# Holding back a load until an earlier load has landed, in a retention and gated feed-forward kernel

## The chip, the cores and the metric

The kernel runs on one core of a Trainium2 chip. The metric is the device time of one execution in microseconds (us), the median of three runs; lower is better. Engines are named as the profile names them: PE (TensorE, its matmuls; PEld are its weight loads), DVE (VectorE), ACT (ScalarE), POOL (GpSimd) and SP (SyncE), which in this kernel issues every transfer. A small q behind an engine's name (SPq) marks its instruction queue: issues and waits that leave the engine itself idle.

## The reference

Two parts, one fed by the other. The first is a linear attention with decay (retention) over 4 batches, 8 heads, 768 tokens and a head dimension of 64:

```python
for t in range(S):
    state = gamma[None, :, None, None] * state + np.einsum('bhd,bhe->bhde', k[:, :, t], v[:, :, t])
    y[:, :, t] = scale * np.einsum('bhd,bhde->bhe', q[:, :, t], state)
```

The second takes that output as `x`, one row of 512 per token:

```python
h = np.maximum(x @ w_in, 0.0)                  # w_in: 512 x 1024
# conv_out: a convolution of h along the sequence, three taps per feature, zero padded
gate = 1.0 / (1.0 + np.exp(-conv_out))
return (h * gate @ w_out).astype(np.float32)   # w_out: 1024 x 512
```

## The kernel before

The retention runs in chunks of 64 tokens: 24 of them (two groups of batches, 12 chunks each), and chunk n computes with one tile `rw[n]` of query, key (in two layouts) and value. `scores/n` multiplies keys by queries on PE, `masked/n` masks the product on DVE, `scale_v/n` scales the values, `mix/n` and `across/n` make the output and the running state on PE, `carry/n` copies the state to the next chunk, `decay/n` finishes the output. Two chunks make a unit of 128 tokens; `x_head`, `x_rest` split its output into two parts, a head rounded to fp32r and a rest, and `mm1/u/f` multiplies a unit by `w_in`. After the convolution and the gate, `mm2` multiplies by `w_out`, and `store` writes the rows.

Weights come as pairs of 32-bit words in 16 loads of 512 KB: `load_w/0` to `load_w/7` bring `w_in`, `load_w/8` to `load_w/15` bring `w_out`, and the small `load_w/16` the taps of the convolution. Each weight is taken apart by a chain of steps on ACT and DVE that begins with `w_abs/i` (ACT, line 481) and `w_clamp/i` (DVE, line 486).

The loads of chunks 0 to 3 are cut in two, `load/n` (query and key, line 335, 512 KB) and `load_kv/n` (key and value, line 339, 512 KB). From chunk 4 on one `load/n` brings 1024 KB. `load_consts` (line 343, 80 KB) and `load_gy` (line 347, 128 KB) bring constants. All loads and stores are issued by SP, in the order in which they stand in a written-out list `ORDER`; an instruction that has to wait on SP keeps all behind it waiting. A load waits for its tile to be free (three tiles `rw`, four tiles `g` for weights). Each transfer signals its landing on one of eight semaphores, DMAHW0 to DMAHW7, taken in turn, and a transfer also waits until the one before it on its semaphore has landed, so that at most eight are in flight. A table `HELD` (line 56) makes seven loads wait for a given compute step as well, `load_kv/2` for `mix/0` and `load_kv/3` for `make_gy/0` among them. PE starts with matmuls on a dummy tile (`fill`, line 318, and `keep_warm`, line 312) while the first loads are on their way.

Of the kernel before, what the change touches and what calls it, by code (L numbers as in the profile page):

```python
# [27 lines left out]
CONV = 2 * NF  # L28
# [20 lines left out]

FILL = 6  # L50
ALONE = 4
SUMMED = 0
BY_SCALAR = (0, 1, 2, 3, 4, 5, 6, 7, 10, 11, 12, 15, 17, 21, 22, 23)


HELD = {
    "load_kv/2": "mix/0", "load_kv/3": "make_gy/0", "load/7": "w_low/4", "load_w/4": "w_abs/3",
    "load_w/6": "w_clamp/5", "load_w/10": "carry/7", "load_w/13": "w_abs/10",
}
# [171 lines left out]
def has_next(n):  # L231
    return ALONE <= n + 1 < N_CHUNKS

# [21 lines left out]
def retention_then_gated_ffn(  # L255
# [36 lines left out]
    def buf(name, shape, dtype=F32):  # L292
        return pool.tile(shape, dtype, **place(name))

    def ps_buf(name, shape=(P, 512)):
        return psum.tile(list(shape), F32, **place(name))


    for i, place_ in enumerate(PLACES.split()):
        name, size = place_.split(":")  # L300
# [7 lines left out]
    def keep_warm(k):  # L308

        ps = ps_buf("ps_o")  # L310
        for i in range(k):
            nc.tensor.matmul(ps[:, : 2 * P], warm, warm.unsqueeze(1).broadcast_to([P, 2, P]), start=True, stop=True)  # L312

    def fill(k):

        ps = ps_buf("ps_o")
        for i in range(k):
            nc.tensor.matmul(ps, warm, warm.unsqueeze(1).broadcast_to([P, 4, P]), start=True, stop=True)  # L318
            made[f"fill/{i}"] = nc.cur_bb.bb.instructions[-1]
# [10 lines left out]
    def load(n):  # L330


        rw[n] = buf("rw", [P, 5, 2, NPAIR, C])
        slots = slice(0, 2 if n < ALONE else 4)
        nc.sync.dma_start(flat(rw[n][:, slots]), qkv[n][:, slots])
# [176 lines left out]
    def w_low(i):  # L512
        low, high, _ = pieces[i]
        out = parts[i] = buf("es", [P, 512], F32R) if i < SUMMED else low.bitcast(F32)
        nc.vector.scalar_tensor_tensor(
# [3 lines left out]
    def w_parts(i):  # L519
        m, es = pieces[i][2], parts[i] if i in parts else None  # L520
        if i < NF:
            fs = slice(i * P, (i + 1) * P)
            m, es = (a if a is None else a.rearrange("p (k f) -> p k f", k=NPAIR) for a in (m, es))
            return wi_hi[:, :, fs], wi_lo[:, :, fs], m, es
        return wo_hi[i - NF], wo_lo.get(i - NF), m, es
# [24 lines left out]
    def w_add(i):  # L550
# [6 lines left out]
        _, lo, m, es = w_parts(i)  # L557
        if i < SUMMED:
            ps = w_ps[i]
# [246 lines left out]
        nc.sync.dma_start(out[r0 : r0 + P, cs], os[u, t, h][:, : cs.stop - cs.start])  # L806

    made = {}
    fill(FILL)
    for name in ORDER.split():  # L810
        if name in WARM:
            keep_warm(WARM[name])
        kind, *args = name.split("/")
        emit[kind](*map(int, args))
        made[name] = nc.cur_bb.bb.instructions[-1]
        if name in HELD:
            tc.add_manual_dep(
                made[name], made[HELD[name]].name,
                mybir.DependencyInfo(mybir.DependencyClass.Sync, mybir.DependencyReason.DATA), reason="held back",
            )  # L820


_OUT = (B * S, DM)
# [48 lines left out]
```

## Time and profile before

| | |
|---|---|
| runs | 334.77, 334.76, 332.27 us; median 334.76 us |
| profiled execution, first to last instruction | 331.0 us |
| PE busy | 322.2 us, 97% of the span |
| DVE busy | 288.7 us, 87% |
| ACT busy | 215.0 us, 65% |
| read from HBM, written to it | 33.79 MB, 6.29 MB |
| TensorE clock granted | full, in every slice |

The page gives the busy time of each engine. The stretches give the same for a part of the span, with the share of the DMA engines. The timeline gives the start and length of single instructions, with the idle time of the engine before them and what ended it. The DMA view, over a short stretch, gives the time from issue to landing of the one transfer issued in it. In the chain of waits each piece is followed back to what released it.

### The profile page before, as it was taken

Reading aid. Unit: us, or ns where it says so; the run is one execution under the profiler, and the core shown is the slowest. Engines: PE = TensorE matmul, PEld = TensorE weight load, DVE = VectorE, ACT = ScalarE, POOL = GpSimd, SP = SyncE. Lnnn points to the kernel's source line nnn. Section 1 sums busy time; section 2 is a strip of 40 time slices with the busy share of each in tenths; the row PEclk is TensorE's granted clock in tenths of the full one; section 3 lists DMA queues with packets and bytes.
Section 4 is the critical chain, followed back from the end, with each engine's and each line's share of the span. In section 5 each row is a group of like instructions: output and inputs, shape, how many; then the busy total and the mean of one; then the engine's idle time right before and its main releaser. Section 6 shows DMA issues by size and latency. Waiting matters only on the chain.

```text
span 331.0 us, 10761 instructions
## 1 busy us (share of the span) xinstructions
PE 322.2 (97%) x4642; PEld 289.4 (87%) x4642; DVE 288.7 (87%) x566; ACT 215.0 (65%) x448; POOL 26.1 (8%) x100
## 2 busy tenths in 40 slices
PE   8888999999999999899999999999999999999996
PEld 3778999999999988798888989999999888987885
DVE  3999999999999999897999998779988887869980
ACT  4657774756666475755939664965796866776761
POOL 0000002003110100300000000021011200120000
PEclk9999999999999999999999999999999999999999
DMA  7999787556443331574150000000000101010111
GB/s 256 386 331 338 251 311 266 197 159 239 180 168 153 130 100 63 160 264 139 51 192 34 34 0 35 34 2 7 25 34 0 64 1 64 3 63 0 65 63 63
DMA packets 10415, 40.77 MB, mean 123 GB/s; under 512 B 1280, under 2 KB 1792, under 8 KB 7808
## 3 DMA queue, kind: packets, MB, share of 16 engines
q1 hardware_dynamic: 10368, 40.09, 34.0%
q8 instruction: 36, 0.59, 0.7%
q14 instruction: 11, 0.09, 0.1%
HBM read 33.79 MB, written 6.29 MB: 121 GB/s over the span
## 4 chain that ended last, share of the span: by engine, by line
PE 94%; DMA 4%; issue 0%; ACT 0%; DVE 0%; ACTq 0%
PE ps_o L793 40%; PE ps_m L576 20%; PE ps_m L696 8%; PE ps_y L696 8%; PE ps_s L396 5%; PE ps_st L396 4%; DMA rw<-in_qkv 4%; PE ps_y L396 4%; PE ps_s L696 3%; PE ps_o L318 2%; PE ps_o L312 0%; ACT rw L364 0%; ACT o_sb L800 0%; DVE o_sb L304 0%; ACTq L800 0%
## 5 line engine op out<-in xcount | busy, mean ns | idle before, releaser
L576 PE MATMUL ps_m<-xu,wi_hi 128*128 128x256 f32 x384 | 68.8, 283 | 0.0
L793 PE MATMUL ps_o<-h,g 128*128 128x512 f32 (+1 forms) x200 | 62.7, 382 | 0.0
L576 PEld LDWEIGHTS ps_m<-xu,wi_hi 128*128 128x128 f32 x384 | 58.4, 189 | 0.9
L576 PE MATMUL ps_m<-xu,wi_lo 128*128 128x256 f32 x192 | 53.5, 279 | 0.0
L764 ACT ACTIVATE cv<-cv 128x512 f32<-128x512 f32 x48 | 29.8, 630 | 34.0 <-DVE cv L758 34.0
L396 PE MATMUL ps_y<-rw 64*64 64x64 f32 x1472 | 48.4, 220 | 0.1
L396 PEld LDWEIGHTS ps_y<-rw 64*64 64x64 f32 x1472 | 45.2, 135 | 0.7 <-ACT rw L629 0.4
L793 PEld LDWEIGHTS ps_o<-h,g 128*128 128x128 f32 x200 | 37.2, 188 | 7.1 <-ACT o_sb L800 0.4
L779 DVE TENSOR_TENSOR g<-cv,g 128x512 fp32r<-128x512 f32 x48 | 32.6, 687 | 8.1 <-ACT g L774 7.4
L758 DVE SCALAR_TENSOR_TENSOR cv<-h,cw_sb,cv 128x256 f32<-128x256 f32 x84 | 38.7, 478 | 1.0 <-ACT cv L753 0.4
L774 ACT CAST g<-cv 128x512 fp32r<-128x512 f32 x48 | 29.3, 617 | 11.7 <-DVE cv L769 10.3
L576 PEld LDWEIGHTS ps_m<-xu,wi_lo 128*128 128x128 f32 x192 | 36.1, 188 | 0.0
L396 PEld LDWEIGHTS ps_s<-rw 64*64 64x64 f32 x768 | 24.4, 135 | 8.6 <-issue 3.2
L396 PE MATMUL ps_s<-rw 64*64 64x64 f32 x768 | 27.6, 221 | 4.0 <-DMA rw<-in_qkv 1.5
L396 PE MATMUL ps_st<-rw 64*64 64x64 f32 x704 | 25.0, 219 | 0.5 <-ACT rw L364 0.5
L364 ACT ACTIVATE rw<-rw,consts_sb 128x128 f32<-128x128 f32 x64 | 20.4, 391 | 6.4 <-DMA rw<-in_qkv 6.4
L396 PEld LDWEIGHTS ps_st<-rw 64*64 64x64 f32 x704 | 22.6, 135 | 1.5 <-ACT rw L364 1.0
L753 ACT ACTIVATE cv<-h,cw_sb 128x256 f32<-128x256 f32 x42 | 20.5, 504 | 2.0 <-DVE g L779 2.0
L800 ACT COPY o_sb<-ps_o 128x512 f32<-128x512 f32 (+1 forms) x25 | 13.9, 561 | 11.8 <-PE ps_o L793 11.7
L423 DVE TENSOR_TENSOR rw<-ps_s,consts_sb 128x512 f32<-128x512 f32 x24 | 16.4, 684 | 5.2 <-PE ps_s L396 5.2
L793 PE MATMUL ps_o<-h_m,g 128*128 128x512 f32 (+1 forms) x50 | 19.1, 384 | 0.0
L793 PE MATMUL ps_o<-h_s,g 128*128 128x512 f32 (+1 forms) x50 | 19.1, 384 | 0.0
(256 smaller groups left out, 758.4 us busy)
## 6 DMA issues: line engine op xcount, KB each, us to landing
rw<-in_qkv SPq DMA_DIRECT2D x20, 1024.0 KB, 5.8
out_y<-o_sb SPq DMA_DIRECT2D x23, 256.0 KB, 2.0
g<-in_w_in SPq DMA_DIRECT2D x8, 512.0 KB, 6.3
rw<-in_qkv SPq DMA_DIRECT2D x8, 512.0 KB, 6.5
g<-in_w_out SPq DMA_DIRECT2D x8, 512.0 KB, 4.7
out_y<-o_sb SPq DMA_DIRECT2D x2, 128.0 KB, 1.7
consts_sb<-in_consts SPq DMA_DIRECT2D x1, 128.0 KB, 8.8
consts_sb<-in_consts SPq DMA_DIRECT2D x1, 80.0 KB, 6.0
```

The costliest lines, as they stand in the source:

```text
L364: nc.scalar.activation(v[:, :, g], v[:, :, g], AF.Copy, scale=by[:, g : g + 1])
L396: nc.tensor.matmul(out, lhsT, rhs, start=start, stop=stop, skip_group_check=True)
L423: nc.vector.tensor_tensor(out=rw[n][:, 1], in0=s_ps[n], in1=mask_sb.unsqueeze(1).broadcast_to([P, 2, NPAIR, C]), op=ALU.mult)
L576: nc.tensor.matmul(h_ps[u, p][:, odd], w[:, k, fs], x[:, k].rearrange("p b t -> p (b t)"), start=(i == 0), stop=(i == len(products) - 1),)
L696: nc.tensor.matmul(ps[:, i], w[k][:, fs], x[:, k].rearrange("p b t -> p (b t)"), start=(i == m == 0 and q in (1, 5)), stop=(m == len(produ ...
L753: nc.scalar.activation(cvs[u, p][:, i], hs[u, p][:, i, :, 1 : P + 1], AF.Copy, scale=cw_sb[:, f, 1:2])
L758: nc.vector.scalar_tensor_tensor(out=cv, in0=h[:, :, k : k + P], scalar=cw_sb[:, f, k : k + 1], in1=cv, op0=ALU.mult, op1=ALU.add)
L764: nc.scalar.activation(cvs[u, p], cvs[u, p], AF.Sigmoid)
L774: nc.scalar.copy(gs[u, p][:, 0], cvs[u, p])
L779: nc.vector.tensor_tensor(out=lo, in0=cvs[u, p], in1=hi.bitcast(F32), op=ALU.subtract)
L793: nc.tensor.matmul(ps, g, w[f][:, cs], start=(f == 0 and i == 0), stop=(f == NF - 1 and i == 2))
L800: nc.scalar.copy(o[:, :n], o_ps[u, t, h][:, :n])
```

## The change

Before a load is issued, SP now also waits for the landing of an earlier load: of the last load that has at least `AHEAD` = 8 units of 128 KB, that is 1 MB, of other loads between itself and the new one. The sizes are in the table `SIZES`: 4 units for 512 KB, 8 for a 1024 KB load, 3 for `load_consts`, 1 for `load_gy`; `load_w/16` counts nothing. Stores are neither held nor counted. The order, the tiles and all other instructions stay.

```diff
+AHEAD = 8
+SIZES = {"load_consts": 3, "load_gy": 1, "load_kv": 4, "load_w": 4, "load": 4}
...
+    def hold(this, by):
+        tc.add_manual_dep(
+            this, by.name, mybir.DependencyInfo(mybir.DependencyClass.Sync, mybir.DependencyReason.DATA),
+            reason="held back",
+        )
+
+    def behind():
+
+        between = 0
+        for load, size in reversed(loads):
+            if between >= AHEAD:
+                return load
+            between += size
...
         if name in HELD:
-            tc.add_manual_dep(
...
+            hold(made[name], made[HELD[name]])
+        if kind in SIZES:
+            landed = behind()
+            if landed is not None:
+                hold(made[name], landed)
+            size = 0 if name == f"load_w/{CONV}" else 8 if kind == "load" and int(args[0]) >= ALONE else SIZES[kind]
+            loads.append((made[name], size))
```

SP at the start of the program, from `load_consts` to `load_kv/2`. Line 343 is `load_consts`, 339 `load_kv`, 463 `load_w`, 335 `load`, 347 `load_gy`; in the changed kernel all numbers are higher by two. DMAHW0 is the landing of `load_w/0`, DMAHW1 of `load_w/1`, and so on in turn. Before:

```order
L343 DMA consts_sb_66<-in_consts 128x160
L339 DMA rw_146<-in_qkv 128x1024
L463 DMA g_2_150<-in_w_in 128x1024
L335 DMA rw_152<-in_qkv 128x1024
L339 DMA rw_152<-in_qkv 128x1024
L347 DMA consts_sb_66<-in_consts 128x256 [waits DMAHW0_49]
L335 DMA rw_156<-in_qkv 128x1024 [waits DMAHW1_49]
L339 DMA rw_156<-in_qkv 128x1024 [waits DMAHW2_49,PE_49]
```

The same place of SP after the change:

```order
L345 DMA consts_sb_66<-in_consts 128x160 [waits DMAHW0_49]
L341 DMA rw_146<-in_qkv 128x1024
L465 DMA g_2_150<-in_w_in 128x1024 [waits DMAHW1_49]
L337 DMA rw_152<-in_qkv 128x1024 [waits DMAHW3_49]
L341 DMA rw_152<-in_qkv 128x1024 [waits DMAHW4_49]
L349 DMA consts_sb_66<-in_consts 128x256 [waits DMAHW5_49]
L337 DMA rw_156<-in_qkv 128x1024
L341 DMA rw_156<-in_qkv 128x1024 [waits DMAHW6_49,DMAHW2_49,PE_49]
```

No row has moved. `load_consts` now waits for `load_w/0`, `load_w/2` for `load_w/1`, `load/1` for `load_consts`, `load_kv/1` for `load_kv/0`, `load_gy` for `load_w/2` (and `load/2` stands behind it), `load_kv/2` for `load/1`.

SP from `load_w/16` to `load_w/5`, before (the names 344 and 450 are `load/4` and `load/5`, 412 and 453 `load_w/4` and `load_w/5`):

```order
L463 DMA cw_t_263<-in_conv_w 128x48 [waits DMAHW5_49]
L339 DMA rw_257<-in_qkv 128x1024 [waits DMAHW6_49,DVE_49]
L335 DMA rw_344<-in_qkv 128x2048 [waits DMAHW7_49,PE_49,Activation_49]
L463 DMA g_0_412<-in_w_in 128x1024 [waits DMAHW0_49,Activation_49]
L335 DMA rw_450<-in_qkv 128x2048 [waits DMAHW1_49,DMAHW2_49,DVE_49,PE_49]
L463 DMA g_1_453<-in_w_in 128x1024 [waits DVE_49]
```

The same place after the change:

```order
L465 DMA cw_t_263<-in_conv_w 128x48 [waits DMAHW2_49]
L341 DMA rw_257<-in_qkv 128x1024 [waits DVE_49]
L337 DMA rw_344<-in_qkv 128x2048 [waits DMAHW3_49,DMAHW7_49,PE_49,Activation_49]
L465 DMA g_0_412<-in_w_in 128x1024 [waits DMAHW6_49,Activation_49]
L337 DMA rw_450<-in_qkv 128x2048 [waits DVE_49,PE_49]
L465 DMA g_1_453<-in_w_in 128x1024 [waits DMAHW0_49,DVE_49]
```

Again no row has moved. `load_w/16` now waits for `load_kv/2` (DMAHW2), and `load_kv/3` stands behind it; `load/4` waits for `load/3` (DMAHW3), `load_w/4` for `load_kv/3` (DMAHW6), and `load_w/5` for `load_w/4` (DMAHW0).

## Rows read from the trace of the kernel before

**Rows 1.** The page, part 1: busy us, share of the span, instructions

```profile
PE 322.2 (97%) x4642; PEld 289.4 (87%) x4642; DVE 288.7 (87%) x566; ACT 215.0 (65%) x448; POOL 26.1 (8%) x100
```

**Rows 2.** Four stretches of the span; the first row names the columns

```profile
core 0: us, PE busy (x) PEld busy (x) DVE busy (x) ACT busy (x) POOL busy (x), PEclk, DMA share, GB/s
10.00:20.00 10.00, 7.65 (x281) 6.62 (x283) 9.35 (x17) 7.81 (x19) 0.00 (x0) 1.00 1.01 371
20.00:26.00 6.00, 4.97 (x123) 4.73 (x117) 5.86 (x12) 2.55 (x8) 0.00 (x0) 1.00 0.99 326
26.00:40.00 14.00, 14.00 (x423) 13.61 (x423) 13.28 (x28) 10.66 (x25) 0.00 (x0) 1.00 0.83 274
40.00:60.00 20.00, 20.00 (x572) 19.42 (x565) 19.50 (x39) 12.45 (x27) 2.06 (x6) 1.00 0.80 294
```

**Rows 3.** The chain of waits, 10 to 32 us: start us, us, what

```profile
11.73 5.07 DMA rw<-in_qkv
...
17.35 8.26 DMA rw<-in_qkv
...
25.75 0.33 PE ps_s L396 x4
```

**Rows 4.** Waits on transfers: who, for what, us in total, times, longest

```profile
ACT rw L364 <- DMA rw<-in_qkv: 6.4, 5, 3.1
ACT m L481 <- DMA g<-in_w_in: 4.6, 4, 2.4
PE ps_s L396 <- DMA rw<-in_qkv: 1.5, 2, 1.0
```

**Rows 5.** Timeline of SP: start us, us, issue of a transfer

```profile
0.74 0.86 SPq L463 DMA_DIRECT2D g<-in_w_in  x2
2.11 0.43 SPq L343 DMA_DIRECT2D consts_sb<-in_consts  x1
3.83 0.45 SPq L335 DMA_DIRECT2D rw<-in_qkv  x1
16.91 0.33 SPq L339 DMA_DIRECT2D rw<-in_qkv  x1
20.19 0.33 SPq L463 DMA_DIRECT2D g<-in_w_in  x1
21.74 0.33 SPq L335 DMA_DIRECT2D rw<-in_qkv  x1
22.12 0.57 SPq L463 DMA_DIRECT2D g<-in_w_in  x1
```

**Rows 6.** DMA view around one issue each: KB, us from issue to landing

```profile
g<-in_w_in SPq DMA_DIRECT2D x1, 512.0 KB, 3.9
consts_sb<-in_consts SPq DMA_DIRECT2D x1, 80.0 KB, 6.0
rw<-in_qkv SPq DMA_DIRECT2D x1, 512.0 KB, 8.1
rw<-in_qkv SPq DMA_DIRECT2D x1, 512.0 KB, 6.2
g<-in_w_in SPq DMA_DIRECT2D x1, 512.0 KB, 6.7
rw<-in_qkv SPq DMA_DIRECT2D x1, 1024.0 KB, 7.6
g<-in_w_in SPq DMA_DIRECT2D x1, 512.0 KB, 8.5
g<-in_w_out SPq DMA_DIRECT2D x1, 512.0 KB, 4.2
g<-in_w_out SPq DMA_DIRECT2D x1, 512.0 KB, 3.3
```

**Rows 7.** Timeline of ACT and of DVE: where the sixth weight block begins

```profile
30.76 0.69 ACT L481 ACTIVATE m<-g 128x512 f32<-128x512 f32 x1
...
31.51 0.42 DVE L486 TENSOR_SCALAR m<-m 128x512 f32<-128x512 f32 x1
```

More of the change, by code (lines that the diff above doesn't have):

```diff
@@ L808, in retention_then_gated_ffn @@
     made = {}
+    loads = []
+    def hold(this, by):
[9 more added lines that the diff above has]
+            between += size
     fill(FILL)
@@ L816, in retention_then_gated_ffn @@
         if name in HELD:
-            tc.add_manual_dep(
-                made[name], made[HELD[name]].name,
-                mybir.DependencyInfo(mybir.DependencyClass.Sync, mybir.DependencyReason.DATA), reason="held back",
-            )
+            hold(made[name], made[HELD[name]])
[5 more added lines that the diff above has]
+            loads.append((made[name], size))
 _OUT = (B * S, DM)
```

## The prediction

> **What bounds the kernel now.** I read the page first, then stretches, the chain of waits, the waits on transfers, and single transfers. The page says that PE is busy 322.2 of 331.0 us [rows 1]: there is little to win but the time in which PE stands. The stretches show where that is: from 10 to 26 us PE works 7.65 of 10 and 4.97 of 6 us, and the DMA engines are at 1.01 and 0.99 of their time; from 26 us on PE is busy throughout and the DMA share falls to 0.83 and 0.80 [rows 2]. The chain agrees: its two pieces of DMA end at 25.6 us, and PE's scores of chunk 4 start behind them at 25.75 [rows 3]. PE waited for transfers twice, 1.5 us in all, once for 1.0 us (the scores of chunk 4); ACT waited 6.4 us for keys and values and 4.6 us for weight blocks [rows 4]. DVE is the second bound: 9.35 of 10, 5.86 of 6, 13.28 of 14 and 19.50 of 20 us [rows 2]. So the kernel is bound by transfers up to 26 us, then by PE with DVE close behind it. What a load loses early stays lost as far as DVE and PE can't catch up.
>
> **What the change adds.** No instruction on PE, DVE, ACT or POOL, no byte, no other order: only waits on SP. I cost SP's waiting itself at nothing. What counts is whether a load that is issued later also lands later.
>
> In the trace loads land in the order of their issue, and under a full queue their issue time doesn't matter: the load of 1024 KB issued at 21.74 lands after 7.6 us, at 29.3, and `load_w/5`, issued at 22.12, after 8.5 us, at 30.6 [rows 5, 6]. That is 1.3 us for 512 KB, the service time. A load could be issued 6 us later and land the same, if its data only stood in the queue. Three loads of 512 KB take 3.8 us of service. With the change a load is issued when the third before it lands, so the three turn around in T, the time from issue to landing with 1 MB in flight; if T is under 3.8 us, nothing is lost.
>
> Which T? The nearest row is `load_kv/2`: held back by `mix/0`, it went out at 11.73 us, when `load/1` (issued 3.83, 8.1 us) was landing at 11.9, so with about 1.1 MB in flight. This is just what the change makes of nearly every early load. It took 5.07 us [rows 3, 5, 6]. `load_kv/3`, issued at 16.91 with 1 MB in flight, took 6.2 us. `load_w/10`, with the 1 MB of `load/10` in flight, took 4.2. With nothing in flight, `load_w/15` took 3.3 and the first load of all 3.9 [rows 5, 6]. So a load that comes late to a working queue takes longer than its share of it; one that is queued early doesn't show this. I take T = 5.1, the row of the same place, between 3.3 and 6.2. Transfer apart, that is 3.8 us of latency under load.
>
> The Trainium skill, page "DMA: Bandwidth & Descriptors", section "Anatomy of one DMA — SWDGE (gpsimd) path", puts a transfer at about 2.0 us fixed plus bytes over 436 GB/s, the fixed part constant; for 512 KB that is an estimate of 3.2 us, and three loads would turn around within their service. By that sum the change costs nothing. The trace agrees for the load on an empty queue (3.3 us) and differs for the one on 1 MB in flight (5.07); the section is also about another issuing path than SP's. The measurement decides.
>
> **The sum.** The longest chain of holds runs from `load_w/0`, landed at 0.74 + 3.9 = 4.6 us, through six loads.
> - `load_consts` is issued at 4.6 instead of 2.11. Its 80 KB take T less 1.1 us of transfer, 4.0: landed 8.6 (before 2.11 + 6.0 = 8.1).
> - `load/1` waits for it: 8.6 + 5.1 = 13.7 (before 11.9, 1.8 us later).
> - `load_kv/2` waits for `load/1`: 18.8 (before 16.8, 2.0 later).
> - `load_w/16` goes with that landing, `load_kv/3` one issue of about 0.5 us behind: 19.3 + 5.1 = 24.4 (before 23.1, 1.3 later; its 6.2 us of before had a delay already).
> - `load_w/4` waits for `load_kv/3`: 29.5 (before 20.19 + 6.7 = 26.9, 2.6 later).
> - `load_w/5` waits for `load_w/4`: 34.6 (before 30.6, 4.0 later).
>
> In general `load_w/5` lands at 4.0 + 6 T. The other chain, `load_w/1`, `load_w/2`, `load_gy`, `load/3`, `load/4`, comes out shorter for `load/4`: 1 MB landed at about 26.4 instead of 25.6. PE arrives later itself by then, so its wait of 1.0 us there is used up; the scores of chunk 4 lose about 1 us.
>
> Who needs `load_w/5`: `w_abs/5` on ACT, which started at 30.76, 0.2 us behind the landing, and took 0.69; `w_clamp/5` on DVE at 31.51 stands behind it [rows 7]. With the block at 34.6, `w_abs/5` ends at about 35.3, and DVE stands 3.8 us later than before. Behind it on DVE, in order, come the second `make_gy` and the mask of the next chunk, for which PE's `mix` waits; behind `w_abs/5` on ACT the first `relu` of the next unit, which frees PE's accumulator. So PE can't run past it. DVE was idle 0.72 us from 26 to 40 and 0.50 from 40 to 60 [rows 2]; these 1.2 us can take up some of it. 3.8 - 1.2 = 2.6 us reach the end.
>
> Later loads: the tiles hold them back already, and `load_w/8`, `load_w/9`, `load_w/14` and `load/16` alone get a later issue. I cost them at nothing: ACT waited for weight blocks four times, at the first, second, fourth and fifth block, and PE twice, the last time at 25.75 [rows 3, 4], so behind these loads stands slack. Without that cover each would cost up to what T exceeds 3.3 by, some 2 us. The stores wait behind the loads on SP but feed nobody.
>
> The span becomes 331.0 + 2.6 = 333.6 us. The median of the runs, 334.76, is 3.8 us above the profiled span (the fastest run 1.3), and 2.6 us on it make 337.4 us, 0.8% slower.
>
> **The rivals.**
> *Hidden.* T is 4.4 or less. With 4.0 + 6 T, `load_w/5` then lands at 30.6 or earlier, as before, and all holds lie under data that stand in the queue. Time 331.0, in the runs 334.8. For it: 4.2 for `load_w/10`, 3.3 on an empty queue [rows 6]. Against it: 5.07 and 6.2 at the very place [rows 3, 6]. The sum of the Trainium skill, above, comes out here.
>
> *Faster.* With less in flight the transfer that is awaited has the DMA engines to itself. `load_kv/3` took 6.2 us while `load/4`, `load_w/4` and the next came in behind it; with T = 4.2 it lands at 17.0 + 4.2 = 21.2 instead of 23.1, and `load/4` two us earlier too. PE's 1.0 us at 25.75 goes: 330.0, in the runs 333.8. It decides the case below T = 4.3. More than 1% needs 3.3 us, and PE's waits on transfers hold 1.5 [rows 4]; only if the runs' spread (332.27 to 334.77) is made by early transfers could more come. Against it: before `load_kv/3`, with more in flight than ever, loads landed 1.3 us apart.
>
> *The start slows down fully.* T = 6.2, the row of `load_kv/3`: `load_w/5` lands at 41.2, 10.6 late, less 1.4 of slack and idle time 9.2 us: 340.2, in the runs 344.0. From T = 5.2 on the loss passes 3.3 us. Against the full figure: when loads land further apart, a late one has more time before its turn, so T falls back.
>
> That the waits are missing is no case: SP's rows show them.
>
> **Chances.** The forecast (0.5 to 3.3 us slower) 0.42; hidden 0.16; faster by less than 1% 0.05, by more 0.05; the start slowed by more than 3.3 us 0.32. A measurement of this kernel tells about 1% from no change. So faster by over 1% 0.05, within 1% 0.63, slower by over 1% 0.32. The range: its low end, 332.8, takes in the hidden case and the faster one (333.8 in the runs) and 1 us of the runs' spread; its high end takes T up to 5.7 (`load_w/5` at 38.2, 7.6 late, 6.2 us at the end, 341.0 in the runs). The forecast's own range is 335.3 to 338.1.
>
> **What would show it.** Right: in the profile of the changed kernel `load/1`, `load_kv/2` and `load_w/5` land at about 13.7, 18.8 and 34.6 us; the DMA share from 10 to 20 us falls from 1.01 to about 0.8; ACT's wait for weight blocks grows from 4.6 us by 3 or more; DVE stands before line 488, the old 486; PE's idle time before 36 us grows by about 2.6. If 512 KB loads with 1 MB in flight land in under 4.4 us, T was too high and the case is *hidden*. If the loads land late and the end doesn't move, DVE and PE had more to give than 1.2 us. If the loss shows after 60 us, one of the four later loads had no cover.

## The result, and the profile after

| | before | changed |
|---|---|---|
| median of four runs beside each other | 334.45 us (332.27 to 334.77) | 337.50 us (336.40 to 337.92) |
| changed / before | | 1.0114, 95% interval 1.0072 to 1.0156 |
| profiled execution | 331.0 us | 335.6 us |

The change makes the kernel slower by 1.1%, 3.8 us by the ratio (2.4 to 5.2), 3.05 us by the medians and 4.6 us by the two profiled executions. The engines run the same instructions. The page of the changed kernel, part 1, against [rows 1]:

```profile
PE 323.6 (96%) x4642; PEld 289.5 (86%) x4642; DVE 288.9 (86%) x566; ACT 214.8 (64%) x448; POOL 27.0 (8%) x100
```

The stretches, with the columns of [rows 2], and one more, from 6 to 10 us, changed and (last row) before:

```profile
10.00:20.00 10.00, 7.43 (x221) 6.06 (x222) 8.26 (x14) 5.43 (x13) 0.00 (x0) 1.00 0.86 295
20.00:26.00 6.00, 4.63 (x155) 4.45 (x151) 4.50 (x9) 3.99 (x11) 0.00 (x0) 1.00 0.89 285
26.00:40.00 14.00, 11.29 (x317) 10.86 (x316) 11.69 (x21) 7.25 (x17) 0.00 (x0) 1.00 0.83 295
40.00:60.00 20.00, 20.00 (x503) 19.41 (x503) 19.86 (x42) 14.23 (x33) 2.06 (x6) 1.00 0.80 285
6.00:10.00 4.00, 4.00 (x40) 2.22 (x39) 2.91 (x7) 1.04 (x2) 0.00 (x0) 1.00 0.82 233
6.00:10.00 4.00, 4.00 (x42) 2.49 (x41) 3.76 (x8) 1.70 (x4) 0.00 (x0) 1.00 0.96 364
```

The DMA engines moved 295 and 285 GB/s from 10 to 26 us where it was 371 and 326, and already from 6 to 10 us only 233 where it was 364. PE is short of work in the stretch up to 40 us, 11.29 of 14 us busy where it was 14.00, and from then on as full as before. From 10 to 40 us it stands 3.3 us more than before; the other 1.3 us of the 4.6 lie in time that the profile counts as busy, 323.6 against 322.2 us. So the loss lies at the start and is then carried along.

The chain of waits of the changed kernel, 5 to 32 us (start us, us, what), against [rows 3]:

```profile
1.17 4.55 DMA g<-in_w_in
...
5.74 6.36 DMA g<-in_w_in
...
12.11 4.61 DMA consts_sb<-in_consts
...
16.79 4.90 DMA rw<-in_qkv
...
21.84 8.46 DMA rw<-in_qkv
...
30.44 0.33 PE ps_s L398 x4
```

These are `load_w/1`, `load_w/2`, `load_gy`, `load/3` and `load/4`, each from the second on issued at the landing of the one above it, and behind them the scores of chunk 4, at 30.44 instead of 25.75. `load/4` itself took 8.46 us, little more than before (8.26, [rows 3]). The scores of chunk 2 were late already; timeline of PE, before and changed:

```profile
16.30 0.27 PE L396 MATMUL ps_s<-rw 64*64 64x64 f32 x2
...
19.31 1.15 PE L398 MATMUL ps_s<-rw 64*64 64x64 f32 x32 [0.96 <-DMA rw<-in_qkv]
```

The waits on transfers, against [rows 4]:

```profile
ACT rw L366 <- DMA rw<-in_qkv: 7.3, 5, 3.5
ACT m L483 <- DMA g<-in_w_in: 7.0, 5, 2.7
PE ps_s L398 <- DMA rw<-in_qkv: 4.1, 3, 2.7
```

PE now waits 4.1 us for query and key instead of 1.5, 2.7 of them for `load/4`. The issues on SP, against [rows 5] (`load_consts`, `load_kv/0`, `load/1`, `load/2`, `load_kv/2`, `load_w/4`, `load_w/5`), and the DMA view of single loads, against [rows 6] (`load_kv/0`, `load_w/2`, `load/1`, `load/2`, `load_kv/2`, `load_w/5`):

```profile
4.49 0.33 SPq L345 DMA_DIRECT2D consts_sb<-in_consts  x1
4.86 0.43 SPq L341 DMA_DIRECT2D rw<-in_qkv  x1
7.22 0.33 SPq L337 DMA_DIRECT2D rw<-in_qkv  x1
12.48 0.43 SPq L337 DMA_DIRECT2D rw<-in_qkv  x1
13.47 0.33 SPq L341 DMA_DIRECT2D rw<-in_qkv  x1
24.96 0.33 SPq L465 DMA_DIRECT2D g<-in_w_in  x1
31.64 0.33 SPq L465 DMA_DIRECT2D g<-in_w_in  x1
```

```profile
rw<-in_qkv SPq DMA_DIRECT2D x1, 512.0 KB, 6.0
g<-in_w_in SPq DMA_DIRECT2D x1, 512.0 KB, 6.4
rw<-in_qkv SPq DMA_DIRECT2D x1, 512.0 KB, 6.2
rw<-in_qkv SPq DMA_DIRECT2D x1, 512.0 KB, 6.7
rw<-in_qkv SPq DMA_DIRECT2D x1, 512.0 KB, 7.0
g<-in_w_in SPq DMA_DIRECT2D x1, 512.0 KB, 4.4
```

`load/2`, the tenth transfer, so landed at 12.48 + 6.7 = 19.2 us. In the kernel before it landed at 5.86 + 9.0 = 14.9, 4.3 us earlier:

```profile
5.86 0.33 SPq L335 DMA_DIRECT2D rw<-in_qkv  x1
```

```profile
rw<-in_qkv SPq DMA_DIRECT2D x1, 512.0 KB, 9.0
```

Where the prediction looked for the sixth weight block, timeline of ACT and DVE, against [rows 7]:

```profile
36.05 0.69 ACT L483 ACTIVATE m<-g 128x512 f32<-128x512 f32 x1 [0.51 <-DMA g<-in_w_in]
...
36.77 0.43 DVE L488 TENSOR_SCALAR m<-m 128x512 f32<-128x512 f32 x1 [0.48 <-ACT m L483]
```

DVE comes there 5.3 us later (36.77 against 31.51), and of that it stands 0.5 us at this place; the rest it brought along.

### The profile page after: what moved, and what is told of

It is laid out like the page before. It is cut to its first block, busy times and chain, and to the rows that moved or that the text cites. A ratio compares the mean times of both kernels' runs of the same rounds, so it can differ in the third digit from the quotient of the medians.

```text
span 335.6 us, 10756 instructions
## 1 busy us (share of the span) xinstructions
PE 323.6 (96%) x4642; PEld 289.5 (86%) x4642; DVE 288.9 (86%) x566; ACT 214.8 (64%) x448; POOL 27.0 (8%) x100
## 4 chain that ended last, share of the span: by engine, by line
PE 90%; DMA 9%; issue 1%; SPq 0%; ACT 0%; ACTq 0%
PE ps_o L795 39%; PE ps_m L578 20%; PE ps_m L698 8%; PE ps_y L698 8%; PE ps_s L398 5%; PE ps_st L398 4%; DMA rw<-in_qkv 4%; PE ps_y L398 4%; DMA g<-in_w_in 3%; PE ps_s L698 3%; DMA consts_sb<-in_consts 1%; SPq L465 0%; ACT o_sb L802 0%; SPq L337 0%; ACTq L802 0%
## 5 line engine op out<-in xcount | busy, mean ns | idle before, releaser
L398 PE MATMUL ps_y<-rw 64*64 64x64 f32 x1472 | 49.1, 220 | 0.0
L366 ACT ACTIVATE rw<-rw,consts_sb 128x128 f32<-128x128 f32 x64 | 20.4, 390 | 7.3 <-DMA rw<-in_qkv 7.3
L755 ACT ACTIVATE cv<-h,cw_sb 128x256 f32<-128x256 f32 x42 | 20.4, 503 | 2.0 <-DVE g L781 2.0
```

The lines of the kernel that those rows point to most:

```text
L366: nc.scalar.activation(v[:, :, g], v[:, :, g], AF.Copy, scale=by[:, g : g + 1])
L398: nc.tensor.matmul(out, lhsT, rhs, start=start, stop=stop, skip_group_check=True)
L755: nc.scalar.activation(cvs[u, p][:, i], hs[u, p][:, i, :, 1 : P + 1], AF.Copy, scale=cw_sb[:, f, 1:2])
```

## The experiments

A hold is a wait of SP for a landing, as the change adds it. Two theories stood against the reading that a chance stall of `load/4` made the loss (B). A: depth. A load that is issued onto 1 MB in flight comes too late, the DMA engines run dry in between. C: waiting on SP costs as such, whatever is in flight. The ratios below are to the kernel before, run beside each; 1% is 3.3 us.

**How much may be in flight.** Three kernels differ from the changed one in one number.

```diff
-AHEAD = 8
+AHEAD = 16      # e1_ahead16: 2 MB in between
+AHEAD = 12      # e7_ahead12: 1.5 MB
+AHEAD = 4       # e2_ahead4: 0.5 MB
```

> The held loads wait as in the changed kernel, but for a load with 2 MB of others in between. Theory A (a load issued onto 1 MB in flight reaches the DMA engines after they have run dry; queue depth is what costs): four loads of 512 KB are still in flight, 5.1 us of service against 5 to 7 us from issue to landing, so nearly nothing is lost: 0 to +1 us on the kernel before, PE idle before 31 us back from 6.6 to about 3.5 us. Theory B (the loss is a chance stall of load/4, which took 8.5 us): unrelated to depth, anything from 0 to +4.6. Theory C (waiting on SP as such costs, since each hold keeps all behind it): nearly as many holds, so +2 to +4 us.

> A load waits for one with 1.5 MB of others in between: four loads of 512 KB in flight at most. Theory A: four loads take 5.1 us of service against 4.5 to 6.5 us from issue to landing, so about a third of the loss: +0.5 to +2 us on the kernel before, between the 2 MB kernel (0.25% above before) and the changed kernel (1.1% above). No other theory puts it between.

> A load waits for one with only 0.5 MB in between, so two loads of 512 KB are in flight instead of three. Theory A: two loads per turnaround of 4 to 5 us, 2.0 to 2.5 us each where 1.3 is the service; load_w/5 lands at 42 to 48 us instead of 36.0, and the time is 6 to 12 us above the changed kernel. Later weight loads (load_w/8, load_w/9, load_w/14) begin to be late too. Theory B: no more than 1 us above the changed kernel. Theory C: about the changed kernel, since the number of holds is the same.

| loads in between | ratio | interval |
|---|---|---|
| 2 MB | 1.0025 | 0.9992 to 1.0059 |
| 1.5 MB | 1.0011 | 0.9979 to 1.0044 |
| 1 MB (the change) | 1.0114 | 1.0072 to 1.0156 |
| 0.5 MB | 1.0362 | 1.0274 to 1.0450 |

With 1.5 and 2 MB the holds are there and cost nothing that can be told; with 1 MB they cost 1.1%, with 0.5 MB 3.6%. That is against C: with 1.5 MB SP did wait, `load/2` was issued at 10.66 instead of 5.86 us and landed at 17.0 instead of 14.9. Against B speak the regular steps, and that `load/4` took hardly longer than before. I had expected 1.5 MB to lose a part; its interval still leaves room for 0.4%. One row of the profiled execution with 0.5 MB says that more than transfers is in the 3.6%: PE was busy 6.06 of 10 us from 10 us on and 4.48 of the next 6, and the granted clock was 0.64 on average in those 6, where it was 1.00 before [rows 2]. All runs with 0.5 MB have a mean granted clock of 0.98 or 0.985, by my estimate at most 5 to 7 us of PE's time out of the 12 us lost.

```profile
20.00:26.00 6.00, 4.48 (x118) 4.32 (x112) 3.63 (x7) 3.41 (x8) 0.00 (x0) 0.64 0.74 235
```

**Which holds.** The holds were limited to a part of the loads, by their place in the order.

```diff
-            if landed is not None:
+            if landed is not None and len(loads) < 10:         # e5_first
+            if landed is not None and 10 <= len(loads) < 19:   # e6_mid
+            if landed is not None and len(loads) >= 19:        # e4_late
+            if landed is not None and len(loads) < 6:          # e10_first_a
+            if landed is not None and 6 <= len(loads) < 10:    # e11_first_b
```

> Only the seven holds from load_consts to load/2 are made; from load_kv/2 on loads are issued as before. In the changed kernel these seven already had load/2 landing 4.3 us later. Theory A (depth): load/2 lands 3 to 4.5 us later than before, the loads behind it queue up deep and catch up a part, +2 to +3.5 us in the end. My prediction's chain put only 1.6 us on load/2: then +1 to +1.5 us. Theory B (the chance stall of load/4 made the loss): 0 to +1.

> Only the nine holds from load_kv/2 to load_w/5 are made; the first ten transfers go out as before, eight in flight. Theory A: up to 14.9 us all loads land as before, then load_w/4 and load_w/5 1 to 3 us later, +1 to +2.5 us in the end. If nearly all of the loss is made here, +3.5 to +4.5, and first holds cost nothing; if none, 0 to +0.5.

> Only the loads from load/6 on are held; the first 19 transfers are issued as before. My prediction's step that the later holds cost nothing: 0, within 0.5 us of the kernel before. Theory C: +1 to +3 us. If load_w/8 or load_w/9 have no cover: +1 to +2 us, with ACT waiting at line 483 after 48 us.

> Only the first three holds are made: load_consts and load_kv/0 on load_w/0, load_w/2 on load_w/1. Theory A (a load that is issued onto 1 MB in flight comes too late, each time anew): these three put load_w/2 1.0 to 1.4 us later, the rest queue up deep behind it and lose no more: +1 to +1.5 us. If the first three make it all, +3.5 to +4.

> Only the four holds on load/1, load_kv/1, load_gy and load/2 are made; the first six transfers go out as before. Theory A: load/2 lands 2 to 3 us later, +1.5 to +3 us in the end; together with the first three holds, the 4 us of all seven.

| holds made | ratio | interval |
|---|---|---|
| `load_consts` to `load/2` (seven) | 1.0120 | 1.0089 to 1.0151 |
| the first three of them | 1.0044 | 1.0012 to 1.0077 |
| the other four | 1.0030 | 0.9991 to 1.0069 |
| `load_kv/2` to `load_w/5` (nine) | 1.0027 | 1.0006 to 1.0048 |
| `load/6` and later | 1.0003 | 0.9968 to 1.0038 |

The first seven holds alone cost as much time as the whole change, 4.0 us, more than the 2 to 3.5 expected. Three of them alone cost 0.4%; for the other four, from which 1.5 to 3 us were expected, the interval takes in no change. In the profiled executions `load/2` landed 2.0 us late with the first three, 3.1 with the other four and 4.5 with all seven, so each group of late loads loses anew, as A says. The next nine alone cost a quarter of a per cent, and the later ones nothing that can be told, as predicted.

The kernel with the late holds alone issues its first 19 transfers as the kernel before does, so its profiled execution is a second trace of that start. `load/2` landed at 15.1 there (14.9 in the kernel before), `load_kv/2` at 17.5 (16.8), `load/4` at 24.9 (25.6), the scores of chunk 2 came at 17.14 (16.30), PE did not wait for `load/4`, and `w_clamp/5` started at 32.65 (31.51). So two executions of one start differ by up to 1.1 us; the 4.3 us of `load/2` are clear of that, differences below 1 us are not.

With the first seven alone the clock fell too; the stretches of that kernel:

```profile
18.00:22.00 4.00, 1.15 (x32) 1.04 (x32) 2.76 (x6) 1.34 (x5) 0.00 (x0) 0.96 1.04 389
22.00:25.00 3.00, 2.96 (x74) 3.00 (x75) 2.56 (x6) 1.98 (x5) 0.00 (x0) 0.50 0.94 381
```

PE was busy 1.15 of 4 us and then got 1.2 instead of 2.4 GHz from 22 to 25 us. All four runs of this kernel have a mean granted clock of 0.993 to 0.995, so by my estimate up to about 2 of its 4.0 us are clock and the rest is late loads. In the profiled execution of the changed kernel this did not happen (1.00 in all stretches above), so it is no part of its 4.6 us; of the changed kernel's four runs one shows 0.995. That the seven holds make the whole loss of the changed kernel is therefore not shown, only that they make half of it or more.

**The disputed cost by itself.** `e3_loads_alone` has no computing, only 36 loads of 512 KB in four series of nine.

```diff
+    for phase, ahead in enumerate((9, 4, 2, 1)):
+        for i in range(9):
...
+            nc.sync.dma_start(t.bitcast(I32), src.bitcast(I32))
+            this = nc.cur_bb.bb.instructions[-1]
+            back = i - ahead - 1
+            if back >= 0:
+                hold(this, made[phase * 9 + back])
+            elif i == 0 and phase:
+                hold(this, made[-1])
```

> Leaves out all computing: 36 loads of 512 KB, in four series of nine, each series begun when the last has landed, then stores of zeros. In the series a load waits for the landing of nothing, then of the load with four, two and one others in between (2 MB, 1 MB, 0.5 MB). Theory A: the first two series take about 13.5 us (nine times 1.26 and 2), the third 15.5 to 18 us, the fourth 18 to 23. If the fixed time per transfer is 2 us whatever is in flight (the Trainium skill's sum), the third takes 13.5 too and the fourth 15. If the third takes 13.5 here and not in the kernel, the computing beside it is what makes loads late, not the depth.

Timeline of SP; the first issue of each series comes when the last load of the series before has landed, and the last load of all, issued at 61.45, took 4.9 us:

```profile
0.73 3.80 SPq L333 DMA_DIRECT2D t<-in_w_in  x8
...
15.47 7.54 SPq L333 DMA_DIRECT2D t<-in_w_in  x8
...
30.25 9.61 SPq L333 DMA_DIRECT2D t<-in_w_in  x8
...
46.09 14.02 SPq L333 DMA_DIRECT2D t<-in_w_in  x8
```

The series, one execution each, took 14.7 us without holds, 14.8 with 2 MB in between, 15.8 with 1 MB and 20.3 with 0.5 MB (13.5 was expected for the first two). So the depth costs something without any computing, but at 1 MB only 1.1 us in nine loads. In the changed kernel `load/2`, the tenth transfer, landed 4.3 us later than before. The kernel's own ten loads were then run alone, four times.

```diff
+    start = [
+        (w_in[0], 1024, 4), (w_in[1], 1024, 4), (qkv_part(0, 0), 1024, 4), (consts[:, 256:], 160, 3),
+        (qkv_part(0, 2), 1024, 4), (w_in[2], 1024, 4), (qkv_part(1, 0), 1024, 4), (qkv_part(1, 2), 1024, 4),
+        (consts[:, :256], 256, 1), (qkv_part(2, 0), 1024, 4),
+    ]
+    for series, ahead in enumerate((100, 8, 12, 8)):
...
+            if series == 3 and n < 1024:
+                continue
```

> Leaves out all computing. The kernel's own first ten loads (load_w/0 to load/2, same sizes and order), four times, each series begun when the one before has landed: with no hold, with the changed kernel's holds (1 MB), with 1.5 MB in between, and with the 1 MB holds but without load_consts and load_gy. Then stores of zeros. In the kernels the ten take 14.1 us from the first issue to the landing of load/2 before the change, and 18.4 us after it. If the DMA engines alone make the loss: about 14, 18, 14.5 us. If the computing beside it does: about 14, 15 to 15.5, 14 (the series of 512 KB loads with 1 MB lost only 1.1 us in nine). If the two small loads, counted as 384 and 128 KB, make the gaps: the fourth series is over 2 us shorter than the second, where their data alone are worth 0.5.

Timeline of SP, the start of each series; the DMA view of `load_kv/0`, `load_w/2`, `load/1`, `load/2` in the second; and its stretch from 5.3 to 9.3 us behind its start (no PE columns):

```profile
0.73 0.86 SPq L342 DMA_DIRECT2D t<-in_w_in  x2
...
14.79 0.80 SPq L342 DMA_DIRECT2D t<-in_w_in  x2
...
29.87 0.80 SPq L342 DMA_DIRECT2D t<-in_w_in  x2
...
44.81 0.80 SPq L342 DMA_DIRECT2D t<-in_w_in  x2
```

```profile
t<-in_qkv SPq DMA_DIRECT2D x1, 512.0 KB, 4.6
t<-in_w_in SPq DMA_DIRECT2D x1, 512.0 KB, 4.9
t<-in_qkv SPq DMA_DIRECT2D x1, 512.0 KB, 5.1
t<-in_qkv SPq DMA_DIRECT2D x1, 512.0 KB, 5.3
```

```profile
20.06:24.06 4.00, 0.00 (x0) 0.00 (x0) 0.00 (x0) 1.00 0.98 356
```

Alone, the ten loads take 14.1 us without holds, 15.1 with those of the change, 14.9 with 1.5 MB. The fourth series, without the two small loads, took 15.9 us. Its last landing ran beside the stores behind it; but its last load was issued 9.7 us after its start, against 9.8 in the second series, so it is not the generous sizes of the small loads that make gaps. Only 1.0 of the 4.3 us shows without computing. The same loads under the same holds took 4.6, 4.9, 5.1 and 5.3 us here and 6.0, 6.4, 6.2 and 6.7 in the kernel; only `load_kv/1` took less there (4.4 against 5.3). And yet without holds, with eight in flight, the computing does not slow them: 14.1 us both here and in the kernel before. Nor did the DMA engines simply run dry. From 6 to 10 us they were busy 0.82 of the time in the changed kernel and moved 233 GB/s, over the same stretch alone 0.98 and 356: they stood more, and a byte also took over a quarter more of their busy time. What the late loads lose, they lose for the most part beside the computing; by what path is not settled. No run tells whether it is the traffic of the engines in the SBUF, the issue of the transfers or their fetches of instructions.

**The other way.** Queue two loads earlier than before, by dropping holds of the kernel before.

```diff
-    "load_kv/2": "mix/0", "load_kv/3": "make_gy/0", "load/7": "w_low/4", "load_w/4": "w_abs/3",
+    "load/7": "w_low/4", "load_w/4": "w_abs/3",                       # e8_free_kv
+    "load_kv/2": "mix/0", "load/7": "w_low/4", "load_w/4": "w_abs/3", # e12_free_kv3
```

> The other way from the kernel before: nothing is held back by a landing, and load_kv/2 and load_kv/3 lose the hold on mix/0 and make_gy/0 too, so they are queued 4 and 3 us earlier. Theory A (a load queued early lands in its turn, one that comes late to 1 MB in flight loses 0.7 and 2.4 us, as these two did): load_kv/2 lands at 16.2 instead of 16.8, load_kv/3 at 20 to 21 instead of 23.2, load/4 at 23 to 24 instead of 25.6; PE's wait of 1.0 us there goes: 0.5 to 1.2 us faster than before. If early loads get in the way of those that are awaited: 0 to 1 us slower.

> The kernel before with the hold of load_kv/3 on make_gy/0 taken away alone (load_kv/2 keeps its own). With both taken away load_kv/3 and load/4 landed 1.7 us earlier and PE's wait of 1.0 us for load/4 was gone, but load_kv/2 landed 0.8 us later and PE waited 1.3 us for it. If that is all that ate the gain: load_kv/2 lands at 16.8 as before, load/4 at 24, and it is 0.5 to 1 us faster than before. If DVE's work is what PE runs into behind it: 0 within 0.3 us, as with both.

1.0004 (0.9978 to 1.0030) with both dropped, 1.0021 (0.9987 to 1.0054) with the second alone: no gain. SP, DMA view (`load_kv/2`, `load_kv/3`, `load/4`), waits and PE with both dropped:

```profile
7.81 0.33 SPq L339 DMA_DIRECT2D rw<-in_qkv  x1
...
13.02 0.43 SPq L339 DMA_DIRECT2D rw<-in_qkv  x1
17.88 0.33 SPq L335 DMA_DIRECT2D rw<-in_qkv  x1
```

```profile
rw<-in_qkv SPq DMA_DIRECT2D x1, 512.0 KB, 9.8
rw<-in_qkv SPq DMA_DIRECT2D x1, 512.0 KB, 8.4
rw<-in_qkv SPq DMA_DIRECT2D x1, 1024.0 KB, 6.0
```

```profile
PE ps_s L396 <- DMA rw<-in_qkv: 0.5, 1, 0.5
```

```profile
17.00 0.62 PE L396 MATMUL ps_y<-rw 64*64 64x64 f32 x14 [1.32 <-issue]
```

`load_kv/3` landed at 21.4 instead of 23.1 and `load/4` at 23.9 instead of 25.6, and PE's wait of 1.0 us for it is gone, as expected; but that wait is missing in the second trace of the old start too. `load_kv/2`, issued 3.9 us earlier, landed at 17.6, no earlier than in the two traces of that start (16.8 and 17.5); and PE stood 1.3 us up to 17.0, for nothing that the profile shows (not for `load_kv/2`, as I wrote in the second expectation: that landed 0.6 us later). With the second hold alone dropped, PE's wait for `load/4` was gone as well, and PE stood 1.5 us up to 19.3, where it stood 1.3 before too, and 1.8 us up to 23.0. One profiled execution can't tell which of these belong to the edit. Both expectations of a gain failed: by the runs, freeing these loads is worth nothing, and no kernel here beats the one before.

## Why the prediction was right, and where it was not

**The time**: 337.4 us was forecast and 337.5 measured, inside the range. That the two meet so closely is partly luck: I added 2.6 us to the old median. The spans differ by 4.6 us, the medians by 3.05, because the profiled execution of before lay 3.5 us under its median and that of the changed kernel only 1.9.

**The bound**, transfers up to 26 us and then PE with DVE: right. PE stood before 40 us and no more than before after that, 3.3 us in all where 2.6 were forecast. The DMA share from 10 to 20 us fell to 0.86 (0.8 forecast); ACT's wait for weight blocks grew by 2.4 us, not by 3 or more.

**The price of being late**: right in kind, a little small in size. T was 5.1; the eleven held loads of 512 KB up to `load_w/5` took 4.1 to 7.0 us, 5.6 on average: 6.0, 6.4 and 6.2 for the first three, 4.4 for the next, 4.4 again for `load_w/5`. One T for all of them was too simple. The constant of the Trainium skill (page "DMA: Bandwidth & Descriptors", section "Anatomy of one DMA — SWDGE (gpsimd) path") would have made no loss (an estimate of 3.2 us for 512 KB); the trace differs from it even without computing, 4.6 to 5.3 us for 512 KB.

**The reason behind that price** was too simple. I laid T to the load in flight alone. Without computing the first ten loads lose 1.0 us; in the kernel they lose 4.3.

**The chain to `load_w/5`**: `load/1` was forecast at 13.7 and landed at 7.22 + 6.2 = 13.4; `load_kv/2` 18.8 and 20.4; `load_w/5` 34.6 and 36.0. Order and holds as forecast. That `load/1` came so near is luck: `load_consts` took 2.7 us and not 4.0, `load/1` 6.2 and not 5.1. The path behind `load_w/5` has support where the early loads were on time: with the nine holds alone it landed 2.4 us late, worth 1.0 us by the prediction's sum, and the runs lost 0.9 (0.2 to 1.6).

**The step that failed** is the sentence on the other chain, `load_w/1` to `load/4`, that it "comes out shorter for `load/4`", 26.4 us. It came out longest: `load_w/2` 6.4 us, `load_gy` 4.6 for its 128 KB, `load/3` 4.9 and `load/4` 8.5 us, landed at 30.3. With T for each step before it, 26.4 leaves `load/4` about 6.4 us, though the kernel before shows 8.26 for this very load [rows 3]. PE did not arrive too late to notice; it waited 2.7 us there. So the scores of chunk 4 lost 4.7 us and not 1, and `load_w/5` cost DVE only 0.5 us where 3.8 were put on it. Only 1.7 of the 4.7 us are the longer wait for `load/4` (2.7 of 4.4 us against the second trace of the old start). The rest was lost by chunk 2, whose scores came at 19.31 instead of 16.30 (17.14), as soon as `load/2` had landed, 4.3 us late. The sum has no term for PE's wait for these first chunks.

**What is made up later**: 1.2 us of DVE's idle time were to take up a part. DVE came to `w_clamp/5` 5.3 us late, the span is 4.6 us longer: 0.7 made up, less than two executions differ by. Together with the size of the first steps this makes the 4.6 us of the trace out of my 2.6.

**The later holds** at nothing: right as far as the runs can tell, 1.0003 (0.9968 to 1.0038).

**The rivals**: *Hidden* and *faster* fell: four of the eleven held loads took 4.4 us or less, but not the first three, and the runs are slower. The case *the start slows down fully* had the mechanism and the sign, but not its figure of 344.0: T did not stay at 6.2 (4.9, 4.4 and 4.1 for `load/3`, `load_w/3` and `load_kv/3`), though `load_w/4`, behind the 1024 KB of `load/4`, took 6.6 again. Slower by over 1% had a chance of 0.32 and the measured 1.1% is at that border.

## What to carry to other kernels

A hold on a landing is free only while enough stays queued behind it: here 1.5 MB of loads in between cost nothing that can be told, 1 MB 1.1% and 0.5 MB 3.6%. Price such a hold by a load of the same kernel that was issued late onto a working queue, not by one on an empty queue and not by loads run alone, and follow every chain of holds to its first reader, the one with the small transfer in it too, and the loads of the first chunks. Freeing a load that is late already need not pay: here two loads landed 1 to 1.7 us earlier and the time stayed.

## What the runs showed of the hardware that was not expected

- The time from issue to landing of 512 KB on SP's queue was 3.3 us with nothing in flight, 4.6 to 5.3 us under the holds of the change without computing, and 4.4 to 7.0 us for the same loads and the next beside the computing (5.3 to 6.6 for `load_kv/0` and `load_w/2` in two other kernels that hold them). A load of 128 KB took 4.4 us without computing and 4.6 beside it. With eight loads in flight 512 KB landed about every 1.3 us, computing or not.
- A stretch of 4 us in which PE was busy 1.15 us was followed by 3 us at a granted clock of 0.50, 1.2 GHz instead of 2.4, though PE worked through them (2.96 of 3 us). Late loads can so cost PE a second time: of the ten runs of `e11_first_b`, the seven with a mean granted clock of 0.993 to 0.995 took 336.0 us on average, the three others 334.6. Which gap does it is not shown: the changed kernel's PE was busy 1.67 of 4 us from 18 to 22 us and kept the full clock.
- PE stood 1.3 us with no releaser in the profile (`issue`) in one kernel that had every early load queued early, and as long once, at 140 us, in the kernel before. What it waited for stays open.
